# A written-out program table for the slots of a fused attention and maxout-FFN kernel, with two more steps' x transposed by DMA

## The chip, the cores and the metric

The kernel runs on one core of one Trainium2 chip. The metric is device time in microseconds of that core, as the median of several runs. Before the change it is 206.61 us (11 runs, 205.76 to 207.94).

## What is computed

Attention over 4 batches, 8 heads, 768 positions and head size 64, followed by a feed-forward layer on the 3072 tokens of 512 features that the attention gives.

```python
scores = q @ k.T / 8                       # per batch and head
keep   = causal                            # retrieval heads (0, 2, 6)
keep   = causal & (first 4 keys | last 64) # all other heads
a = softmax(where(keep, scores, -1e9)); x = a @ v
h = max(x @ w1, x @ w2, x @ w3); out = h @ w_out    # 512 -> 768 -> 512
```

Inputs and output are float32; the kernel computes in float16 with float32 accumulation.

## The kernel before, in words

**Steps and slots.** The 768 positions of a batch are two halves of 384, and the 8 heads are two groups of four. A step `t` (0 to 15) is one batch, one half of the queries and one group of heads: batch 0 has steps 0 to 3, and steps 2 and 3 are its second half. A half's scores are laid out in two or four PSUM-sized pieces `u` (`UNITS`); a slot is one `(t, u)`, so a first-half step has two slots and a second-half step four, 48 in all. Slots 0 to 3 belong to the opening; slots 4 to 47, and three more without scores, run in the loop at the end of the function.

**What a slot needs.** `scores` (L403) multiplies keys and queries on TensorE into PSUM, ScalarE takes the exponential into `pt` (L449), and `masks` (L456) multiplies the partly kept blocks on GpSimd (L472). In batch 0 the keys and queries are cast, turned on TensorE and copied (`cast_pair`, `turn_pair`, L159); from batch 1 on they are loaded as float32 by GpSimd's DMA queue (`load`, L171) and turned by VectorE's stream transpose (`turn`, L187, four for each head group). `prep_v` (L383) makes the float16 values: a cast to `va` (L389, on a chosen engine) and a product with the head flags to `vf` (L391, on GpSimd). `av` (L476) makes one pair of heads of a step: 12 or 30 small matmuls (L488), a reciprocal and a scaling on VectorE (L496, L498), which give `x`. FFN matmuls need `x` turned into `xT`: for the steps in `BY_DMA` (4 to 14) `av` issues a transposing DMA from SyncE (L507), for the others `turn_x` (L513) takes three TensorE transposes (L520) and a copy (L524).

**The FFN as a filler.** When the last `x` of a half is issued, `turn_x` appends `ffn(b, half)` (L316) to a queue. That is a generator of 24 units: 18 of four matmuls each (L335, 128x384 out of `yy`), evicted by ScalarE (L343) or combined by VectorE's maximum (L346), and six half units of the output product (L361, copy L367, store L368 by SyncE). `fill(n)` takes `n` units off the queue. There are eight such FFNs.

**What sets the order.** The schedule is manual: each engine runs its instructions in the order in which the Python emits them, and so do the DMA queues of SyncE, ScalarE and GpSimd. `put` files a call under a slot and a place (0: ahead of the scores, "x": behind them, 1: between the two fills, 2: at the end), and the loop emits scores, calls and `pace(n)` units, half of them ahead of place 1. `sync_after` (L195) is a tiny DMA on SyncE that reads slot 8's `pt`; the value loads of batch 1, emitted behind it, therefore wait for that exponential.

**The opening.** Ten dummy matmuls (`idle_work`, L222) run while the first loads land; then steps 0 and 1 are done by hand, and four plus one units of the first FFN between them. Of the four weights, `load_weight` puts `w0t` to GpSimd's queue first, then the second half's first keys and queries, `w1t`, the others, `w2t`, the values, and `woutt`.

Of the kernel before, what the change touches and what calls it, by code (L numbers as in the profile page):

```python
# [1 line left out]

# [9 lines left out]
ALU = mybir.AluOpType  # L13
# [35 lines left out]
def kernel(  # L49
# [14 lines left out]
    nc = tc.nc  # L64
# [18 lines left out]
    NQ = H // G  # L83
    NT4 = B * 2 * NQ

    BY_DMA = range(NQ * 2, NT4 - 1)

    consts = ctx.enter_context(tc.tile_pool(name="consts", bufs=1))
    stage = ctx.enter_context(tc.tile_pool(name="stage", bufs=3))
# [14 lines left out]
    def where(t):  # L104
        bh, qd = divmod(t, NQ)
        return bh // 2, bh % 2, qd
# [25 lines left out]
    def cast_pair(half, hp, engines):  # L132
        cast[half, hp] = []
        for nm, src, op in zip(("kn", "qn"), staged.pop((half, hp)), engines):
            x = half16.tile([P, HB, 2, D], FP16, tag=nm, name=nm)
            op(out=x, in_=src.rearrange("p h j d -> p j h d"))
            cast[half, hp].append(x)
# [6 lines left out]
    def turn_pair(half, hp, *engines):  # L144
        if (0, hp // 2) not in KQs:
            KQs[0, hp // 2] = qkt.tile([P, 2, S, 2], FP16, tag="KQ", name="KQ")
        xs = cast.pop((half, hp))
        n = 2 // len(engines)
        for part, op in enumerate(engines):
            tr = bank([P, 1024], FP16, "tr")  # L150
            for i in range(n):
                for j in range(HB):
                    c = i * HALF + j * P
                    nc.tensor.transpose(
                        tr[:, c : c + P],
                        xs[part + i][:, j].rearrange("p h d -> p (h d)"),
                        ident,
                    )
            op(  # L159
                out=of_pair(hp)[  # L160
                    :, part : part + n, half * HALF : (half + 1) * HALF
                ].rearrange("p i (t j) -> p i t j", j=HB),
                in_=tr[:, 0 : n * HALF].rearrange("p (i j t) -> p i t j", i=n, j=HB),
            )
# [57 lines left out]
    def idle_work(n):  # L222
        sink = sps.tile([P, 2, 512], FP32, tag="st", name="st")
        for _ in range(n):
            nc.tensor.matmul(sink[:, 0, :], zero[:, 0:P], zero, start=True, stop=True)
# [41 lines left out]
    def read_flags():  # L267
        nc.vector.tensor_scalar(
            out=RT1, in0=ir32[:, 0 : 2 * H : 2], scalar1=0.0, scalar2=None,
            op0=ALU.not_equal,  # L270
        )
# [108 lines left out]
                queue.pop(0)  # L380


    def prep_v(t, i, op=None):  # L383
        b, half, qd = where(t)
        vs = staged_v[b, half]
        j, k0 = b % 2, half * HB
        hs = slice(4 * qd + 2 * i, 4 * qd + 2 * i + 2)
        vdst = va[j][:, hs, k0 : k0 + HB, 0:D]
        (op or nc.vector.tensor_copy)(out=vdst, in_=vs[:, hs])  # L389
        k0, k1 = ((0, 1), (1, 4))[half]  # L390
        nc.gpsimd.tensor_tensor(  # L391
            out=vf[j][:, hs, k0:k1, 0:D],
            in0=vs[:, hs, 0:1] if half == 0 else va[j][:, hs, k0:k1, 0:D],
            in1=far[:, hs, k0:k1].unsqueeze(3).to_broadcast([P, 2, k1 - k0, D]),
            op=ALU.mult,
        )
# [6 lines left out]
    def scores(t, u, pairs=(0, 1)):  # L403
# [43 lines left out]
        for x, st in sts.items():  # L447
# [5 lines left out]
            if not early:  # L453
                masks(t, i, u)

    def masks(t, i, u):  # L456
        b, half, qd = where(t)
        pt = pts[t, i]
        h0 = 4 * qd + 2 * i
        for at, u0, nu, cols, n, m0 in MASKED[half]:  # L460
            if at != u:
                continue
            m = mk[:, h0 : h0 + 2, m0 : m0 + n]
            if nu == 1 and len(cols) == 1:
                x = pt[:, u0, :, cols[0] : cols[0] + n]
            elif nu == 2:
                x = pt[:, u0 : u0 + 2, :, cols[0] : cols[0] + n]
                m = m.unsqueeze(1).to_broadcast([P, 2, 2, n])
            else:
                x = pt[:, u0].rearrange("p h (c n) -> p h c n", n=n)[:, :, 0:4:3]  # L470
                m = m.unsqueeze(2).to_broadcast([P, 2, 2, n])
            nc.gpsimd.tensor_tensor(out=x, in0=x, in1=m, op=ALU.mult)  # L472

    xs = {}

# [52 lines left out]
            queue.append(ffn(b, half))  # L528


    SLOTS = [(t, u) for t in range(NT4) for u in range(len(UNITS[where(t)[1]]))]

    def idle():
        idle_work(3)

    dve, act, pool = nc.vector.tensor_copy, nc.scalar.copy, nc.gpsimd.tensor_copy
    idle_work(8)
    read_flags()
    cast_pair(0, 0, (dve, act))
    head_flags()  # L540
    idle_work(2)
    head_masks(0, True)
    turn_pair(0, 0, dve, dve)
    cast_pair(0, 1, (pool, act))
    head_masks(1, True)
    turn_pair(0, 1, dve)
    cast_pair(0, 2, (act, pool))
    scores(0, 0, (0,))
    turn_pair(0, 2, dve)
    scores(0, 0, (1,))  # L550
    head_masks(2, True)
    scores(0, 1, (0,))
    cast_pair(0, 3, (pool, pool))
    load_weight(0)
    far_flags()
    turn_pair(0, 3, dve)
    head_masks(3, True)
    scores(0, 1, (1,))
    scores(1, 0, (0,))
    scores(1, 0, (1,))  # L560
    scores(1, 1, (0,))
    for i in range(2):
        prep_v(0, i, pool)
    for i in range(2):
        prep_v(1, i, dve)
    load_pairs(1, 0, 2, (nc.gpsimd, nc.gpsimd))
    av(0, 0)
    scores(1, 1, (1,))
    av(0, 1)
    load_weight(1)  # L570
    load_pairs(1, 2, 2, (nc.gpsimd, nc.gpsimd))
    av(1, 0)
    turn_x(0, 0, act)
    turn_x(0, 1, act)
    av(1, 1)
    turn_x(1, 0)
    load_weight(2)
    load_v(0, 1, (nc.gpsimd,) * HB)
    load_weight(3)
    turn_x(1, 1)  # L580
    for hp in range(2):
        cast_pair(1, hp, (dve, act))
    fill(4)
    for hp in range(2):
        turn_pair(1, hp, dve)
    for hp in range(NHP):
        head_masks(hp)
    fill(1)


    FIRST = 4
    work = {}

    def put(n, place, f, *args):
        work.setdefault((n, place), []).append(lambda: f(*args))

    for b in range(B):
        o = 12 * b
        for i in range(2):
            if b > 0:  # L600
                put(o + i, 2, prep_v, 2 * NQ * b, i, act if b == 1 else None)
                put(o + 2 + i, 2, prep_v, 2 * NQ * b + 1, i, act if b == 1 else None)
                put(o + i, 1, av, 4 * b - 1, i)
                put(o + 1 + i, "x", turn_x, 4 * b - 1, i)
                put(o + 2 + i, 1, av, 4 * b, i)
                put(o + 3 + i, "x", turn_x, 4 * b, i)
                put(o + 4 + i, 1, av, 4 * b + 1, i)
                put(o + 5 + i, "x", turn_x, 4 * b + 1, i)
            late = 1 if b == 0 else 0
            put(o + (8 if late else 6) + i, late, prep_v, 4 * b + 2, i, act if b == 0 else None)  # L610
            put(o + 10 + i, 2, prep_v, 4 * b + 3, i, act if b == 0 else None)
            put(o + 8 + late + i, 1, av, 4 * b + 2, i)
            put(o + 9 + late + i, "x", turn_x, 4 * b + 2, i)
        if b + 1 < B:
            put(o + (5 if b == 0 else 3), 0, load, b + 1, 0)
            put(o + (8 if b == 0 else 5), 0, load, b + 1, 1)
            if b == 0:
                put(9, 0, lambda: sync_after(pts[3, 1][0:1, 0, 0, 0:2]))
            put(o + (9 if b == 0 else 7), 0, load_v, b + 1, 0)
            put(o + 11, 0, load_v, b + 1, 1)  # L620
            for qd in range(2):
                for x in range(2):
                    for p in range(2):
                        if b == 0:
                            n, place = 10 + 2 * qd + x, "x" if qd else (0, "x")[p] if x == 0 else 0
                        else:
                            n, place = o + 8 + 2 * qd + x, 1
                        put(n, place, turn, b + 1, qd, x, p)
    for i in range(2):
        put(12 * B + i, 1, av, NT4 - 1, i)  # L630
        put(12 * B + 1 + i, "x", turn_x, NT4 - 1, i)
        put(5, 1, cast_pair, 1, 2 + i, (dve, act))
        put(6 + i, 1, turn_pair, 1, 2 + i, dve)

    def pace(n):
        return 2.4 if n < 8 else 1.6 if n < 11 else 3.0 if n < 14 else 3.6 if n < 20 else 4.0

    due = 0.0
    for n in range(FIRST, len(SLOTS) + 3):
        def do(place):  # L640
            for f in work.pop((n, place), ()):
                f()

        do(0)
        if n < len(SLOTS):
            scores(*SLOTS[n])
        do("x")
        due += pace(n)
        part = int(due / 2)
        fill(part)  # L650
        due -= part
        do(1)
        part = int(due)
        fill(part)
        due -= part
        do(2)
    assert not work
    while queue:
        fill(1)
# [33 lines left out]
```

## Time and profile before

| | |
|---|---|
| median of 11 runs | 206.61 us (205.76 to 207.94) |
| the profiled execution | 207.26 us, with a span of 205.5 us from first to last instruction |
| busy: TensorE, VectorE, ScalarE, GpSimd | 191.6, 126.6, 124.9, 128.9 us |
| granted TensorE clock | 1.00 |
| read from HBM, written | 25.17 MB, 6.29 MB |
| stores of the output, from issue to landing | 2.4 us (median of 23) |

The page adds up busy time by engine, follows the chain of work that ended last back from the end, and lists groups of instructions by source line with their mean duration and with what ended the idle time before them. Matmuls overlap in the array, so the mean duration of one (326 ns for 128x384) is not its pitch: in the timeline groups of four start 0.65 us apart. A row such as `xT<-x` names the tile written and the tile read.

### The profile page before, as it was taken

How to read it: one execution, taken by the hardware profiler on the slowest of the kernel's cores; microseconds unless marked ns; L12 is line 12 of the kernel's file. 1: busy time of each engine (PE TensorE's matmuls, PEld its weight loads, DVE VectorE, ACT ScalarE, POOL GpSimd, SP SyncE). 2: the span in 40 equal slices, each digit the busy share in tenths (PEclk: the TensorE clock that was granted, in tenths of full speed). 3: DMA queues.
4: the chain of work that ended last, by engine and by line, in shares of the span. 5: the costliest groups of instructions: out<-in, count | busy, mean ns of one | idle time of the engine just before them, and what ended most of it. 6: DMA issues, size and time to landing. Idle time of an engine off the chain costs nothing.

```text
span 205.5 us, 5167 instructions
## 1 busy us (share of the span) xinstructions
PE 191.6 (93%) x2071; PEld 108.4 (53%) x2071; DVE 126.6 (62%) x257; ACT 124.9 (61%) x190; POOL 128.9 (63%) x156
## 2 busy tenths in 40 slices
PE   7698699888899999999999999999899999999992
PEld 2455354546465456455656466465455465665552
DVE  3886687597656538994696268983546234753540
ACT  3492797868586865746657676656377775514221
POOL 3489569869997834489987906589908816800000
PEclk9999999999999999999999999999999999999999
DMA  5989999999539993803389952603211130012004
GB/s 184 251 130 213 243 245 214 211 221 242 161 56 196 140 249 92 153 3 92 124 149 187 177 184 48 129 19 122 72 22 38 60 117 19 3 51 105 0 0 153
DMA packets 41581, 26.08 MB, mean 127 GB/s; under 512 B 31894, under 2 KB 36566, under 8 KB 41558
## 3 DMA queue, kind: packets, MB, share of 16 engines
q1 hardware_dynamic: 35542, 14.62, 31.8%
q0 software_dynamic: 4784, 10.23, 26.1%
q10 hardware_dynamic: 1232, 0.92, 1.4%
q8 instruction: 16, 0.26, 0.5%
q14 instruction: 7, 0.06, 0.1%
HBM read 25.17 MB, written 6.29 MB: 153 GB/s over the span
## 4 chain that ended last, share of the span: by engine, by line
PE 67%; DMA 19%; DVE 8%; POOL 2%; issue 1%; ACT 1%; ACTq 0%; SPq 0%; POOLq 0%; DVEq 0%
PE yy L335 35%; PE yy L361 13%; PE st L438 8%; PE oacc L488 8%; DMA kq<-in_k_dram 7%; DVE KQ L187 5%; DMA w1t<-in_moe_w_dram 4%; PE yst L335 3%; DMA qs<-in_q_dram 3%; DMA vs<-in_v_dram 3%; DMA xT<-x 2%; DVE x L498 1%; PE yst L361 1%; POOL vf L391 1%; DVE acc L346 1%
## 5 line engine op out<-in xcount | busy, mean ns | idle before, releaser
L472 POOL TENSOR_TENSOR pt<-pt,mk 128x512 f16<-128x512 f16 x84 | 89.7, 1094 | 29.1 <-ACT pt L449 27.8
L449 ACT ACTIVATE pt<-st 128x1024 f16<-128x1024 f32 (+3 forms) x99 | 83.0, 894 | 27.7 <-PE st L438 25.5
L346 DVE TENSOR_TENSOR acc<-yy,acc 128x384 f16<-128x384 f32 x45 | 25.2, 561 | 23.4 <-PE yy L335 17.1
L335 PE MATMUL yy<-xT,w0t 128*128 128x384 f16 x180 | 36.6, 326 | 1.0 <-DMA xT<-x 1.0
L335 PE MATMUL yy<-xT,w2t 128*128 128x384 f16 x180 | 36.6, 326 | 0.0
L335 PE MATMUL yy<-xT,w1t 128*128 128x384 f16 x180 | 36.3, 326 | 0.1
L361 PE MATMUL yy<-woutt,hT 128*128 128x512 f16 (+1 forms) x138 | 32.7, 375 | 0.3 <-DVE hT L346 0.3
L343 ACT CAST acc<-yy 128x384 f16<-128x384 f32 x45 | 21.4, 482 | 18.2 <-PE yy L335 12.3
L438 PE MATMUL st<-KQ 32*128 32x384 f16 (+5 forms) x560 | 28.8, 279 | 1.8 <-DVE KQ L187 1.0
L346 DVE TENSOR_TENSOR hT<-yy,acc 128x384 f16<-128x384 f32 x45 | 25.1, 558 | 6.0 <-PE yy L335 3.4
L488 PEld LDWEIGHTS <-pt 128*128 128x128 f16 x672 | 24.9, 97 | 5.8 <-issue 1.0
L187 DVE STREAM_TRANSPOSE KQ<-kq 128x384 f32<-128x384 f32 x24 | 25.0, 1138 | 0.5 <-DMA kq<-in_k_dram 0.5
L488 PE MATMUL oacc<-va,pt 128*128 128x65 f16 x352 | 25.1, 193 | 0.0
L335 PEld LDWEIGHTS <-w1t 128*128 128x128 f16 x192 | 17.5, 97 | 14.0 <-issue 3.5
L496 DVE RECIPROCAL rc<-oacc 128x6 f32<-128x6 f32 x32 | 6.1, 191 | 30.4 <-PE oacc L488 30.1
L335 PEld LDWEIGHTS <-w2t 128*128 128x128 f16 x192 | 17.3, 98 | 12.2 <-issue 1.4
L335 PEld LDWEIGHTS <-w0t 128*128 128x128 f16 x192 | 17.5, 97 | 11.5 <-issue 0.9
L438 PEld LDWEIGHTS <-KQ 32*128 32x128 f16 (+1 forms) x560 | 12.1, 93 | 21.8 <-issue 15.6
L488 PE MATMUL oacc<-vf,pt 128*128 128x65 f16 x320 | 21.4, 193 | 0.7 <-POOL vf L391 0.7
L367 ACT COPY ot<-yy 128x512 f32<-128x512 f32 x22 | 13.0, 590 | 14.7 <-PE yy L361 13.9
L361 PEld LDWEIGHTS <-hT 128*128 128x128 f16 x150 | 13.4, 98 | 15.0 <-issue 1.4
L391 POOL TENSOR_TENSOR vf<-va,far 128x384 f16<-128x384 f16 x16 | 13.2, 827 | 11.6 <-DVE va L389 9.5
(67 smaller groups left out, 130.3 us busy)
## 6 DMA issues: line engine op xcount, KB each, us to landing
out_dram<-ot SPq DMA_DIRECT2D x23, 256.0 KB, 2.4
vs<-in_v_dram SPq DMA_DIRECT2D x21, 256.0 KB, 4.8
kq<-in_k_dram POOLq DMA_DIRECT2D x6, 384.0 KB, 6.8
kq<-in_q_dram POOLq DMA_DIRECT2D x6, 384.0 KB, 8.5
qs<-in_q_dram ACTq DMA_DIRECT2D x4, 192.0 KB, 5.7
ks<-in_k_dram SPq DMA_DIRECT2D x4, 192.0 KB, 4.9
w0t<-in_moe_w_dram POOLq DMA_DIRECT2D x1, 768.0 KB, 7.1
ks<-in_k_dram POOLq DMA_DIRECT2D x2, 384.0 KB, 6.9
```

What stands on the lines that cost most here:

```text
L187: nc.vector.transpose(out=dst.rearrange("c (p j) -> c j p", j=n)[:, j0:j1], in_=src.rearrange("c (j i) -> c j i", i=R),)
L335: nc.tensor.matmul(yy[:, 0:HALF], w_t[wi][:, ks, ni * P : (ni + 1) * P], xT[b, half][ks].rearrange("p a t -> p (a t)"), start=(ks == 0), s ...
L343: nc.scalar.copy(out=acc[ni], in_=yy[:, 0:HALF])
L346: nc.vector.tensor_tensor(out=dst, in0=yy[:, 0:HALF], in1=acc[ni], op=ALU.max)
L361: nc.tensor.matmul(yo[:, 0:n], hT[ns][:, tb * P : (tb + 1) * P], woutt[:, ns, c : c + n], start=(ns == 0), stop=(ns == NNB - 1),)
L367: op(out=ot[:, c : c + n], in_=yo[:, 0:n])
L391: nc.gpsimd.tensor_tensor(out=vf[j][:, hs, k0:k1, 0:D], in0=vs[:, hs, 0:1] if half == 0 else va[j][:, hs, k0:k1, 0:D], in1=far[:, hs, k0:k ...
L438: nc.tensor.matmul(sts[g // m][:, g % m, c0 : c0 + n * P], KQ[rows, 0, ki * P : (ki + 1) * P], KQ[rows, 1, t0 : t0 + n * P], start=(c0 == ...
L449: nc.scalar.activation(out=pts[t, i][:, u, h0 : h0 + m, 0:w], in_=st[:, :, 0:w], func=AF.Exp, scale=sc,)
L472: nc.gpsimd.tensor_tensor(out=x, in0=x, in1=m, op=ALU.mult)
L488: nc.tensor.matmul(o[:, qi, hl, 0 : D + 1], pt[:, u, hl, c : c + P], vv[:, 2 * hp + hl, ki, 0 : D + 1], start=(idx == 0), stop=(idx == len ...
L496: nc.vector.reciprocal(out=rc, in_=o[:, :, :, D])
```

## The change

A literal table takes the place of `put` and `pace`: one row for each slot from 4 on, with its FFN units, a flag, and four lines of calls (ahead of the scores, behind them, between the fills, at the end). With the flag the scores of the two head pairs are emitted apart, with a third of the units between them if that comes to a whole one. Most rows repeat the former places with calls moved by a slot or less. `BY_DMA` now holds steps 2 and 15 too. `prep_v` takes an engine for each of its two operations, and three masks go to VectorE. The opening's casts, flags and values are spread over the engines in another way, both scores of steps 0 and 1 stand ahead of the first `av`, and seven units instead of five are taken in it.

```diff
-    BY_DMA = range(NQ * 2, NT4 - 1)
+    BY_DMA = (2, 4, 5, 6, 7, 8, 9, 10, 11, 12, 13, 14, 15)
...
-        (op or nc.vector.tensor_copy)(out=vdst, in_=vs[:, hs])
+        op(out=vdst, in_=vs[:, hs])
-        nc.gpsimd.tensor_tensor(
+        vf_engine.tensor_tensor(
...
+    MASK_ON_DVE = ((3, 1, 3), (6, 0, 1), (7, 0, 1))
-            nc.gpsimd.tensor_tensor(out=x, in0=x, in1=m, op=ALU.mult)
+            engine = nc.vector if (t, i, u) in MASK_ON_DVE else nc.gpsimd
+            engine.tensor_tensor(out=x, in0=x, in1=m, op=ALU.mult)
...
     idle_work(8)
+    cast_pair(0, 0, (act, act))
     read_flags()
-    cast_pair(0, 0, (dve, act))
     head_flags()
-    idle_work(2)
     head_masks(0, True)
     turn_pair(0, 0, dve, dve)
+    idle_work(2)
     cast_pair(0, 1, (pool, act))
...
-    cast_pair(0, 2, (act, pool))
+    cast_pair(0, 2, (pool, pool))
...
+    turn_pair(0, 3, dve)
     far_flags()
-    turn_pair(0, 3, dve)
-    head_masks(3, True)
+    prep_v(0, 0, dve, nc.gpsimd)
     scores(0, 1, (1,))
+    prep_v(0, 1, dve, nc.vector)
+    prep_v(1, 0, dve, nc.vector)
     scores(1, 0, (0,))
+    scores(1, 1, (0,))
+    prep_v(1, 1, dve, nc.gpsimd)
+    load_pairs(1, 0, 2, (nc.gpsimd, nc.gpsimd))
     scores(1, 0, (1,))
-    scores(1, 1, (0,))
-    for i in range(2):
-        prep_v(0, i, pool)
-    for i in range(2):
-        prep_v(1, i, dve)
-    load_pairs(1, 0, 2, (nc.gpsimd, nc.gpsimd))
+    scores(1, 1, (1,))
     av(0, 0)
-    scores(1, 1, (1,))
+    load_weight(1)
     av(0, 1)
...
+    PROGRAM = (
+        (2.4, True, "", "", "cast 1 2 dd", "cast 1 3 ap"),
+        (2.4, False, "load 1 0", "", "", ""),
+        (2.0, False, "pair 1 2", "", "", "pair 1 3"),
+        (2.2, False, "load 1 1", "", "", ""),
+        (2.2, True, "", "", "v 2 0 dd", "gate"),
+        (1.6, True, "v 2 1 ap, load_v 1 0", "", "av 2 0", ""),
+        (1.6, True, "", "x 2 0, turn 1 0 0 0, turn 1 0 0 1", "av 2 1, turn 1 0 1 1", "v 3 0 pp"),
+        (3.0, False, "turn 1 0 1 0, load_v 1 1", "x 2 1", "", "v 3 1 ap"),
+        (3.6, False, "", "turn 1 1 0 0, turn 1 1 0 1, turn 1 1 1 1, av 3 0", "", "v 4 0 pd"),
+        (3.0, False, "av 3 1", "", "", "turn 1 1 1 0, v 4 1 ad"),
+        (3.6, False, "x 3 0, x 3 1", "", "av 4 0", ""),
+        (3.6, False, "", "v 5 0 ad, x 4 0, av 4 1", "", "v 5 1 ap, load 2 0"),
...
+        (3.6, False, "av 7 0, x 7 0, av 7 1", "", "", "v 8 1 dp"),
+        (4.0, False, "", "v 9 0 dp", "av 8 0, x 7 1", ""),
...
+        (4.0, False, "", "", "av 11 0", "v 12 0 dp"),
+        (4.2, False, "x 11 0, av 11 1", "", "", "v 12 1 dp"),
+        (4.8, False, "", "v 13 0 dp, x 11 1", "av 12 0", ""),
...
+        (4.0, False, "", "", "av 15 0", ""),
+        (4.0, False, "x 15 0, av 15 1", "", "", ""),
+        (4.0, False, "", "x 15 1", "", ""),
+    )
...
+    for (units, apart, *lines), slot in itertools.zip_longest(PROGRAM, SLOTS[FIRST:]):
+        run(lines[0])
+        if slot and apart:
+            scores(*slot, (0,))
+            part = int(due + units / 3)
+            fill(part)
+            due -= part
+            scores(*slot, (1,))
+        elif slot:
+            scores(*slot)
+        run(lines[1])
+        due += units
         part = int(due / 2)
         fill(part)
         due -= part
-        do(1)
+        run(lines[2])
         part = int(due)
         fill(part)
         due -= part
-        do(2)
+        run(lines[3])
```

In a row, `d`, `a` and `p` stand for VectorE, ScalarE and GpSimd; `v 4 0 pd` is `prep_v(4, 0)` with the cast on GpSimd and the product on VectorE, `pair` is `turn_pair`, `x` is `turn_x`, and `gate` is `sync_after`.

## The prediction

> **What bounds the kernel now.** I read the page's busy times first, then busy time by stage, then what each engine waited for, and last the chain of waits and single stretches of the timeline.
>
> ```profile
> PE 191.6 (93%) x2071; PEld 108.4 (53%) x2071; DVE 126.6 (62%) x257; ACT 124.9 (61%) x190; POOL 128.9 (63%) x156
> ```
>
> TensorE is busy for 93% of the span; nothing else passes 63%. The four stages below are mine: 18 us is where the first FFN unit starts, 53 us where the second FFN does, 198 us where the last output product begins. In each row the second number is the length; TensorE's busy time follows, and the last three are clock, DMA share and GB/s.
>
> ```profile
> 0.00:18.00 18.00, 13.97 (x142) 7.43 (x143) 12.97 (x37) 10.11 (x18) 10.69 (x26) 1.00 0.85 190
> 18.00:53.00 35.00, 29.86 (x343) 16.82 (x341) 25.51 (x49) 25.51 (x40) 28.36 (x33) 1.00 1.10 232
> 53.00:198.00 145.00, 143.86 (x1566) 81.96 (x1567) 87.12 (x170) 87.74 (x130) 89.81 (x99) 1.00 0.46 95
> 198.00:205.50 7.50, 3.89 (x24) 2.15 (x22) 0.98 (x3) 1.55 (x3) 0.00 (x0) 1.00 0.29 105
> ```
>
> So from 53 to 198 us TensorE lacks only 1.1 us; there an edit pays only if it takes work or that 1.1 us off TensorE. From 18 to 53 us it lacks 5.1 us, while the DMA engines are full (share 1.10, 232 GB/s). The first 18 us lack 4.0, of which 1.26 is the start. The last row is not touched.
>
> ```profile
> PE tr L520 <- DVE x L498: 1.7, 4, 0.6
> PE tr L154 <- ACT acc L343: 1.6, 1, 1.6
> PE tr L154 <- POOL kn L136: 1.6, 1, 1.6
> ...
> PE yy L335 <- DMA xT<-x: 1.0, 1, 1.0
> ```
>
> The waits are many and short, and only one of them, 1.0 us for a transposed x, lies behind 53 us. What fixes the 53 us is the chain of waits there:
>
> ```profile
> 25.56 15.02 DMA kq<-in_k_dram
> ...
> 40.60 1.14 DVE KQ L187
> ...
> 44.02 2.00 DVE KQ L187 x2
> ...
> 50.07 2.00 DVE KQ L187 x2
> ...
> 52.99 0.34 PE tr L520 x3
> ```
>
> The keys of batch 1, issued at 25.56, land at 40.58 behind everything queued ahead of them; VectorE turns them, with small work between, until 52.06, and then step 3's last x is turned and the second FFN begins (53.17 in the timeline). From there TensorE has work without end. So the new time is: when that FFN starts, plus what TensorE has left to do, plus its stalls.
>
> **Part 1, the opening (up to 18 us).** GpSimd loses two value casts (0.56 and 0.58) and two of four products ahead of the second half's loads, so these can be issued about 1.2 us sooner than 15.15. But in 14 to 16 us the DMA share is already 1.16, and `w0t` is ahead in the same queue until 17.4; `w0t` itself still waits for the last casts, whose input lands at about 9.3. Only small holes (shares 0.93 and 0.91 in 16 to 18 and 20 to 22 us) can be filled: 0.3 us of 1.2. VectorE gains two casts (0.57 each) and two products; its chain of four casts, two products and four scalings of 0.72 moves the first FFN unit from 18.06 to about 18.9. That is hidden: TensorE next stands until 22.51 for ScalarE, whose evictions are queued behind casts waiting for loads that land at about 21.1. Without that cover it costs 0.9. The two further FFN units taken there end at one that needs `w1t` (landing 25.3): TensorE may wait about 0.8 us in front of the scores, where it idled before anyway. The parted scores change nothing on TensorE: its new order shows no unit between the pairs in any of the flagged slots.
>
> **Part 2, slots 4 to 13.** The total of TensorE is the same, less six transposes of step 2. GpSimd's cast of the last queries now stands ahead of the issue of batch 1's keys and holds it until those land, some 2 us; the keys wait 15.0 us in a full queue, so it costs nothing until the delay nears that. The second group's loads are issued two masks (2 x 1.16) sooner into the same full queue: nothing. On VectorE, between the keys' landing and the second FFN stand now: eight turns of 1.02 (8.2), three pairs of reciprocal and scaling (2.1), one mask, two products, two xT copies of 0.38 (0.8). The mask has no row on VectorE; its nearest are the head-mask builds (0.33 to 0.59 for 512 elements), a product is about 0.3 by the same rows for 128 elements. The sum is 12.3 us, against 12.0 of work and 1.1 of idle before: 40.6 + 12.3 = 52.9 for 53.4 before, less up to 0.3 from the loads.
>
> One rule speaks against the mask and the products on VectorE. The Trainium skill, page "SBUF — State Buffer", section "SBUF: two separate sides", says that VectorE with two SBUF inputs and GpSimd hold one port pair exclusively, for a whole instruction. By it each such operation can wait for a GpSimd mask of 1.16: three of them between 40 and 53 us make 52.9 into up to 56.4. No row of two SBUF inputs on VectorE beside a busy GpSimd exists here; the nearest, value casts on VectorE, took 0.565 on average against 0.51 at least while GpSimd was 63% busy. I take 0.1 each and keep 3.5 for the range.
>
> Step 2's x goes through SyncE's queue, behind the batch-1 values, which landed at 50.08 (ScalarE's cast waited for them), with a store between its two transposes. At 1.19 us a transpose (its issue) and 1.0 for 256 KB at 250 GB/s the second lands at 50.1 + 1.2 + 1.0 + 1.2 = 53.5, less 0.3. The second FFN's second matmul needs it: about 53.1, against 53.33 before. Between 52.6 and 53.1, I take a start earlier by 0.4. The bounds are 1.7 earlier and 3 later; see the rivals.
>
> **Part 3, from the second FFN on.** The one stall:
>
> ```profile
> 142.86 0.65 PE L335 MATMUL yy<-xT,w0t 128*128 128x384 f16 x3
> 144.47 0.32 PE L335 MATMUL yy<-xT,w0t 128*128 128x384 f16 x1 [0.96 <-DMA xT<-x]
> ```
>
> The fourth matmul of a new FFN waited for step 11's last x: its `av` ended at 139.39, and only 3.5 us of other work (two output products, one score slot, one short `av`) stood between. In the new order this gap holds a short score slot, one FFN unit, three output products, a score slot and a short `av`: 0.6 + 0.65 + 3 x 1.29 + 0.66 + 0.37 = 6.2 us for a need of about 5.0. Also, two stores no longer stand ahead of the transposes in SyncE's queue. Gain 1.0. Step 7's gap grows from 3.6 to 5.5 in the same way.
>
> Step 15's x no longer takes six TensorE transposes: three start within 0.17, so 6 x 0.057 = 0.34, and I take 0.3. Here a page says more: "TensorE: Matmul & The Clock Gate", section "PE-mode transpose", gives about 275 ns in a kernel. That would make 1.65 us; but 219 ns is this trace's duration too, and what the queue behind pays is the pitch, 0.057. The DMA in their place needs 0.8 for VectorE and 2.3 to 3.3 to land (those of step 14), under 4.5 + 0.5 us of units and products still ahead. Without that cover it would cost 3 us.
>
> Small gaps between units in this stage, evictions that come late, sum to 1.6 us beside the stall. The turns of batches 2 and 3 are now mostly one at a time, not in pairs that keep VectorE for 2.1 us; masks of steps 6 and 7 leave GpSimd, value casts swap engines at equal price (0.51 to 0.57). I take 0.4 of 1.6, between 1.0 lost and 1.0 gained. Loads and stores keep their order to within a slot, and nothing idles for them there.
>
> **Sum.** The profiled execution took 207.26 (span 205.5 and 1.76 around it). 0.4 + 1.0 + 0.3 + 0.4 = 2.1 gives 205.2; it lay 0.65 above the median of 206.61, so the median becomes 204.5.
>
> **The rivals.** *The opening runs ahead:* the loads do move by 1.2 us and VectorE has no idle, so the second FFN starts 1.6 us sooner: 203.2. For it: the new VectorE chain has no wait in it. Against: a DMA share of 1.10. *The stalls move:* pacing that starves or overfills TensorE elsewhere takes back the stall's 1.0 and the 0.4, and the opening gives nothing: 206.3. *Slower, step 2's transposes land late:* next to software-queue loads a transpose took 9.9 us to land, not 2.4:
>
> ```profile
> xT<-x SPq DMA_TRANSPOSE x1, 9.9
> ```
>
> Issued at about 47 us after the store, the second would land at 57, and the second FFN would start 3.6 us later: 206.6 - 1.7 + 3.6 = 208.5. It decides from a landing past 55, where it eats the other 1.7. Against it: the software queue's loads were through by 47.2, and what is ahead then is counted above. *The change does nothing on TensorE:* excluded but for the parted scores, since the emitted order differs throughout.
>
> **How the numbers follow.** A measurement here tells about 0.3% (0.6 us) from no change. Forecast 204.5 (own range 203.4 to 205.7): 0.54; ahead, 203.2: 0.16; stalls move, 206.3: 0.17; late, 208.5: 0.13. Of the third about a fifth is faster by over 0.6. So faster 0.73, within 0.14, slower 0.13. The range, 202.8 to 207.0, leaves out most of the late case and the far end of the early one.
>
> **What would show it.** Right: the second FFN's first unit at 52.3 to 53.2 us; no wait of `yy` for `xT<-x` near 143 us; no L520 rows of steps 2 and 15; from 53 us on the same TensorE work with less than 1 us idle. Part 2 wrong: `yy` waiting on `xT<-x` near 53 us, or VectorE masks of over 1 us. Part 3 wrong: idle TensorE ahead of the last FFN, near 183 us. The forecast fails if that second start moves by over 1.5 us either way.

## The result, and the profile after

The changed kernel took 203.89 us (median of 12 runs, 202.67 to 205.44) against 206.61 (47 runs beside the changed kernel): a ratio of 0.9881, 95% interval 0.9856 to 0.9907. Executions that lie more than 1.5% above the fastest of their kernel (three of e1, one of e6) are left out of all ratios and medians of the experiments. The profiled execution of the changed kernel took 203.81 us, with a span of 202.1.

The profile after, busy times (share of the span, instructions):

```profile
PE 190.0 (94%) x2059; PEld 108.7 (54%) x2059; DVE 130.4 (65%) x260; ACT 124.8 (62%) x188; POOL 125.6 (62%) x151
```

The same four stages as before (start:end and length, then TensorE, its weight loads, VectorE, ScalarE, GpSimd, clock, DMA share, GB/s):

```profile
0.00:18.00 18.00, 14.51 (x144) 7.81 (x145) 13.07 (x39) 10.39 (x19) 10.77 (x25) 1.00 0.95 208
18.00:53.00 35.00, 30.20 (x343) 17.03 (x340) 27.80 (x52) 24.34 (x36) 27.24 (x31) 1.00 1.04 219
53.00:198.00 145.00, 144.78 (x1574) 83.64 (x1573) 89.14 (x168) 89.71 (x134) 87.54 (x97) 1.00 0.48 100
198.00:202.10 4.10, 0.52 (x5) 0.22 (x3) 0.42 (x1) 0.32 (x1) 0.00 (x0) 1.00 0.40 140
```

TensorE has 12 instructions fewer, the transposes of steps 2 and 15. Behind 53 us it lacks 0.2 us, not 1.1, and by 198 us only 5 matmuls are left instead of 24. What TensorE waited for, longest first (total, times, longest):

```profile
PE tr L525 <- DVE x L503: 1.8, 4, 0.6
PE yy L336 <- DMA w1t<-in_moe_w_dram: 1.5, 1, 1.5
...
PE oacc L493 <- POOL pt L477: 0.8, 1, 0.8
PE st L439 <- DVE KQ L188: 0.7, 1, 0.7
```

The wait of `yy` for `xT<-x` is gone; instead the first FFN's w1t units wait 1.5 us, far ahead of the second FFN. The start of that FFN in TensorE's timeline:

```profile
50.73 0.34 PE L525 MATMUL tr<-ident,x 128*128 128x128 f16 x3 [0.55 <-DVE x L503]
51.77 0.63 PE L439 MATMUL st<-KQ 32*128 32x384 f16 x16 [0.70 <-DVE KQ L188]
52.34 0.83 PE L336 MATMUL yy<-xT,w0t 128*128 128x384 f16 x4
```

52.34 us, for 53.17 before. What comes last ahead of it is still VectorE: the scores at 51.77 waited 0.70 us for the last turn of batch 1's keys and queries (`KQ`). The kernel before has the same wait of 0.7, with one for VectorE's `x` behind it. The chain of waits that ends last, though, passes this place through GpSimd's masks, and reaches TensorE at the next `av`, 1.0 us behind the FFN's first matmul:

```profile
45.93 1.29 POOL pt L477
...
52.18 1.12 POOL pt L477
53.35 0.45 PE oacc L493 x9
```

So VectorE sets the start in both kernels, and GpSimd's masks follow it closely.

The span can be split at the second FFN's start. Before: 53.17 to it and 152.3 behind it. After: 52.34 and 149.8. So 0.8 us of the 3.4 come ahead of it and 2.6 behind, where the number of matmuls is nearly the same (1589 before, 1587 after). The table gives both parts for every kernel; they are of one profiled execution, while the median is of all. The kernel before and e5, e6 and e10 have equal code up to there, and yet they started this FFN anywhere from 51.50 (e6) to 53.17 us (before), so a start of one execution settles little. The length behind it is the steadier number. Where a clock is named in the table, TensorE ran at half of it for a while behind the start, and the figure is what that lost.

| kernel | second FFN at | from there to the end | median us |
|---|---|---|---|
| before | 53.17 | 152.3 | 206.61 |
| after | 52.34 | 149.8 | 203.89 |
| e1, after with the old opening | 53.27 | 149.4 | 204.89 |
| e2, before with the new opening | 51.14 | 153.6 | 206.85 |
| e5, earlier `av` on before | 53.14 | 151.2 | 205.76 |
| e6, single turns on before | 51.50 | 151.4 | 205.41 |
| e10, e5 and e6 | 51.78 | 151.1 | 205.78 |
| e9, after with the old pace | 50.86 | 152.1, 1.5 by the clock | 205.0 |
| e11, after with all masks on GpSimd | 52.78 | 150.8, 1.2 by the clock | 205.16 |
| e4, after with step 2 on TensorE | 52.39 | 150.5, 1.5 by the clock | 205.86 |
| e7, after with the gap filled | 52.00 | 149.8 | 203.43 |
| e8, e4 with the gap filled | 52.76 | 149.1 | 204.56 |

### The profile page after: what moved, and what is told of

Read it like the earlier page. It is cut to its first block, busy times and chain, and to the rows that moved or that the text cites. A ratio compares the mean times of both kernels' runs of the same rounds, so it can differ in the third digit from the quotient of the medians.

```text
span 202.1 us, 5148 instructions
## 1 busy us (share of the span) xinstructions
PE 190.0 (94%) x2059; PEld 108.7 (54%) x2059; DVE 130.4 (65%) x260; ACT 124.8 (62%) x188; POOL 125.6 (62%) x151
## 4 chain that ended last, share of the span: by engine, by line
PE 76%; DMA 8%; POOL 7%; DVE 3%; ACT 2%; issue 1%; SPq 1%; DVEq 0%; ACTq 0%
PE yy L336 41%; PE yy L362 13%; PE st L439 9%; PE oacc L493 9%; DMA w1t<-in_moe_w_dram 5%; POOL pt L477 4%; PE yst L336 3%; DMA ks<-in_k_dram 3%; POOL vf L392 1%; ACT pt L450 1%; DMA out_dram<-ot 1%; DVE KQ L160 1%; PE yst L362 1%; DVE mk L293 1%; ACT ot L368 1%
## 5 line engine op out<-in xcount | busy, mean ns | idle before, releaser
L477 POOL TENSOR_TENSOR pt<-pt,mk 128x512 f16<-128x512 f16 (+1 forms) x81 | 86.6, 1093 | 31.3 <-ACT pt L450 31.3
L336 PE MATMUL yy<-xT,w0t 128*128 128x384 f16 x180 | 36.1, 327 | 0.1
L493 PEld LDWEIGHTS <-pt 128*128 128x128 f16 x672 | 23.8, 97 | 5.5 <-issue 1.4
L503 DVE TENSOR_TENSOR x<-oacc,rc 128x384 f16<-128x384 f32 x32 | 17.8, 558 | 1.1
```

Source lines behind the costliest of these rows:

```text
L336: nc.tensor.matmul(yy[:, 0:HALF], w_t[wi][:, ks, ni * P : (ni + 1) * P], xT[b, half][ks].rearrange("p a t -> p (a t)"), start=(ks == 0), s ...
L477: engine.tensor_tensor(out=x, in0=x, in1=m, op=ALU.mult)
L493: nc.tensor.matmul(o[:, qi, hl, 0 : D + 1], pt[:, u, hl, c : c + P], vv[:, 2 * hp + hl, ki, 0 : D + 1], start=(idx == 0), stop=(idx == len ...
L503: nc.vector.tensor_tensor(out=x, in0=o[:, :, :, 0:D], in1=rc.unsqueeze(3).to_broadcast([P, HB, 2, D]), op=ALU.mult,)
```

## The experiments

The theory at the start was that of the prediction: the stall near 143 us and the small gaps behind 53 us give about 1.4 us, the opening little. The rival was that the opening leads, and that what lies behind it follows from there. Later two more questions came up: what the table's unit counts do, and why the granted clock halves in some executions.

**e1: the changed kernel with the old opening.** Slots 4 on are as in the changed kernel.

```diff
-    cast_pair(0, 0, (act, act))
     read_flags()
+    cast_pair(0, 0, (dve, act))
...
-    prep_v(0, 1, dve, nc.vector)
-    prep_v(1, 0, dve, nc.vector)
     scores(1, 0, (0,))
+    scores(1, 0, (1,))
     scores(1, 1, (0,))
...
+    for i in range(2):
+        prep_v(0, i, pool, nc.gpsimd)
+    for i in range(2):
+        prep_v(1, i, dve, nc.gpsimd)
```

> The changed kernel with the opening of the kernel before (all up to slot 4), table and DMA steps as changed. Theory (most of the gain lies behind 53 us; the opening moves the second FFN's start by 0.8 us at most, and the later slots' work on VectorE and GpSimd sets that start in any case): about 204.3, 0.4 above the changed kernel. Rival (the opening's earlier loads made the 0.8 us and more): 205 or above, with the second FFN's first unit at 53.2 us or later.

Ratio 0.9921 (0.9884 to 0.9958), median 204.89 us: 1.0 more than the changed kernel. The intervals of the two ratios overlap, and of the executions at a clock of 0.996 or more the medians are 204.31 and 203.66, which is 0.65. In its profile the second FFN began at 53.27, 0.9 later, and behind it the length is 149.4, for 149.8 after. So inside this change the opening is worth some 0.6 to 1.0 us, between the two expectations, and not clear of the noise. What is lost lies ahead of the second FFN.

**e2: the kernel before with the new opening alone**, the opposite edit.

> The kernel before with the changed opening alone; slots from 4 on, their paces and the DMA steps as before. Theory: 206.2, 0.4 below the kernel before, the second FFN's first unit between 52.7 and 53.2 us, and the wait of 1.0 us for the transposed x near 143 us still there. Rival (the opening does it): 205.0 or less.

Ratio 1.0015 (0.9992 to 1.0039): nothing. TensorE's waits behind 50 us in e2:

```profile
PE oacc L488 <- POOL pt L472: 1.2, 2, 1.0
PE yy L335 <- DMA xT<-x: 1.0, 1, 1.0
PE st L438 <- DVE KQ L187: 0.2, 1, 0.2
```

The FFN began at 51.14, but TensorE then stood 1.2 us (at 53.0 and 60.6) for GpSimd's masks, a wait that the kernel before has nowhere behind 50 us, and the stall near 143 us is still there. In this execution a lead of 2.0 us came down to 0.8 in the span, and in the median nothing is left. That the new order of the slots behind is what keeps the lead in the changed kernel fits e1 and e2, and is not shown by itself.

**e3: step 15 back on TensorE**, `BY_DMA` without 15.

> The changed kernel with step 15's x turned by TensorE again. By the pitch of a TensorE transpose (0.057 us, six of them): 0.3 us more, 204.2. By the skill's 275 ns each: 1.6 us more, 205.5. If the two copies on VectorE also hold up evictions: up to 0.8 more.

Median 204.0 of 6 (202.88 to 205.02), ratio 0.9874 (0.9832 to 0.9916), against 203.89: 0.1, not told from nothing. The three executions at a clock of 0.997 and above took 202.88 to 203.20; those of the changed kernel at such a clock have a median of 203.66. So the 1.65 of the 275 ns rule is excluded. The 0.3 predicted is too small to be seen or excluded in six executions.

**e4: step 2 back on TensorE**, `BY_DMA` without 2.

> The changed kernel with step 2's x turned by TensorE again. Theory (VectorE's chain between 40 and 52 us sets the start of the second FFN; two copies of 0.38 us more stand on it): 0.4 to 0.8 us more, 204.3 to 204.7. Rival (the transposing DMAs behind the values were the limit of that start): the same or up to 0.5 us less.

205.86 us, ratio 0.9976 (0.9948 to 1.0004), 2.0 more than the changed kernel, and every one of 12 executions had a mean clock of 0.983 to 0.992. Busy time of the engines by the microsecond in e4; the clock is the third number from the end:

```profile
48.00:49.00 1.00, 0.14 (x6) 0.00 (x0) 1.00 (x3) 0.91 (x2) 1.00 (x3) 1.00 1.21 282
49.00:50.00 1.00, 0.31 (x3) 0.17 (x3) 0.95 (x5) 0.58 (x2) 1.00 (x2) 1.00 1.09 220
50.00:51.00 1.00, 0.37 (x4) 0.17 (x3) 0.97 (x2) 0.00 (x0) 1.00 (x3) 1.00 1.21 249
51.00:52.00 1.00, 0.31 (x8) 0.22 (x12) 1.00 (x2) 0.00 (x0) 1.00 (x2) 1.00 0.88 251
52.00:53.00 1.00, 1.00 (x18) 0.43 (x7) 0.66 (x3) 0.45 (x1) 1.00 (x1) 0.52 0.18 51
53.00:54.00 1.00, 1.00 (x10) 0.66 (x9) 0.00 (x0) 1.00 (x2) 0.49 (x2) 0.50 0.00 0
54.00:55.00 1.00, 1.00 (x13) 0.66 (x11) 0.41 (x2) 0.86 (x2) 1.00 (x2) 0.50 0.00 0
55.00:56.00 1.00, 1.00 (x6) 0.54 (x5) 0.54 (x2) 0.00 (x0) 1.00 (x2) 0.77 0.00 0
```

TensorE is busy for 0.14 to 0.37 of each microsecond from 48 to 52, then it gets half the clock for 3.4 us (0.48 + 0.50 + 0.50 + 0.23 lost is 1.7 us), just when the second FFN fills it. One such stretch makes a mean clock of 0.99, as in this execution; in the seven executions at 0.983 two fit, as in e11's trace, which has 6.8 us at half clock. Which part of the 2.0 is the transposes and which the clock, e7 and e8 tell apart.

**e7: the changed kernel with the gap filled.** Eight dummy matmuls of 128x512, whose results nothing reads, go in front of, between and behind the transposes of step 3 (the lines that define `idle` are left out here).

```diff
-        (3.0, False, "av 3 1", "", "", "turn 1 1 1 0, v 4 1 ad"),
-        (3.6, False, "x 3 0, x 3 1", "", "av 4 0", ""),
+        (3.0, False, "av 3 1", "", "", "turn 1 1 1 0, v 4 1 ad, idle 2"),
+        (3.6, False, "x 3 0, idle 3, x 3 1, idle 3", "", "av 4 0", ""),
```

> The changed kernel with eight dummy 128x512 matmuls, which compute nothing used, where TensorE waits between 48 and 52 us (two behind the scores of slot 13, three behind each turned x of step 3). Theory of the clock: TensorE's clock is halved for 3.4 us in those executions in which that stretch looked idle, at 1.5 to 1.7 us each, in about half of them; filled, every execution keeps a clock of 0.997 or more there, and the median falls from 203.9 to 203.4 with a narrower spread. Rival (the clock falls for another reason, or the dummies delay the work): clocks of 0.99 remain, or 0.3 to 0.6 us more.

203.43 us (202.63 to 203.82), ratio 0.9818 (0.9781 to 0.9854), with a clock of 0.996 to 1.0 in all six. Of the changed kernel's own 12 executions four had 0.988 to 0.990 and took 205.08 to 205.44, the other eight a median of 203.66. None of six against four of twelve could still be chance; e8 settles it.

**e8: e4 with the same dummies.**

> Step 2's x on TensorE as in the earlier run (205.86, clock 0.983 to 0.992 in all 12 executions), with the same eight dummy matmuls. Theory of the clock: 203.6 to 204.2 with a clock of 0.997 or more, so that step 2's DMA is worth at most 0.5 us by itself and the rest was the clock. Rival (the turned x itself costs 2 us on VectorE or TensorE): 205.5 or more, with a clock of 1.0.

204.56 us, ratio 0.9889 (0.9849 to 0.9928), clock 0.998 and above in all. The same stretch in e8:

```profile
48.00:49.00 1.00, 0.98 (x11) 0.26 (x10) 1.00 (x2) 0.60 (x2) 1.00 (x3) 1.00 0.92 224
49.00:50.00 1.00, 0.01 (x1) 0.01 (x1) 0.95 (x4) 0.88 (x2) 1.00 (x1) 1.00 1.18 265
50.00:51.00 1.00, 1.00 (x7) 0.42 (x8) 0.96 (x4) 0.00 (x0) 1.00 (x3) 1.00 1.12 218
...
53.00:54.00 1.00, 1.00 (x18) 0.74 (x17) 0.02 (x1) 1.00 (x2) 0.63 (x2) 1.00 0.01 2
```

With work in it the stretch keeps the clock, in six of six where e4 lost it in twelve of twelve. So of e4's loss 1.3 us are the clock (205.86 - 204.56), and with the gap filled step 2's DMA is worth 1.1 (204.56 - 203.43). The two make more than e4's 2.0 because the changed kernel itself loses 0.46 where the gap is open. TensorE's waits from 40 to 60 us in e8 and then in e7:

```profile
PE tr L525 <- DVE x L503: 1.4, 2, 1.0
PE st L439 <- DVE KQ L188: 0.4, 1, 0.4
```

```profile
PE oacc L493 <- POOL pt L477: 0.8, 1, 0.8
```

1.8 us against 0.8. Only 0.4 of the 1.8 is the wait of step 2's own transposes, the first of these rows; the second row is step 3's, which TensorE takes in both kernels:

```profile
43.33 0.34 PE L525 MATMUL tr<-ident,x 128*128 128x128 f16 x3 [0.40 <-DVE x L503]
49.99 0.34 PE L525 MATMUL tr<-ident,x 128*128 128x128 f16 x3 [1.02 <-DVE x L503]
```

VectorE's `x` comes later there: in e8 VectorE also copies step 2's `xT` (0.34 at 46.03), and the mask ahead of that took 1.05 us for 0.58 in the changed kernel. The second FFN starts at 52.76 for 52.00. How the 1.1 divides between copy and mask is not shown.

**e5: the kernel before with step 11's and step 7's last `av` ahead of the scores of its slot.**

```diff
-                put(o + i, 1, av, 4 * b - 1, i)
+                put(o + i, 0 if i and b > 1 else 1, av, 4 * b - 1, i)
```

> The kernel before with one move: in batches 2 and 3 the second pair's av of the last step of the batch before (steps 7 and 11) stands ahead of the slot's scores, not behind the first fill, so that 5.5 us of other work instead of 3.5 covers its transposing DMA. Theory: the wait of 1.0 us near 143 us goes and nothing takes its place: 205.7, 0.9 to 1.0 below the kernel before. Rival (the wait moves to the next thing): within 0.3 of the kernel before.

205.76 us, ratio 0.994 (0.9915 to 0.9965), 1.08 under the kernel before: the stall's size. No wait of TensorE is left behind 60 us.

**e6: the kernel before with the turns of batches 2 and 3 one at a time.**

```diff
-                            n, place = o + 8 + 2 * qd + x, 1
+                            n, place = o + 8 + 2 * qd + x, (1, 2)[p]
```

> The kernel before with the eight stream transposes of each of batches 2 and 3 taken one at a time, one behind the first fill of a slot and one at its end, not in pairs. Theory (the small gaps of 0.15 to 0.2 us between FFN units come from pairs that hold VectorE for 2.1 us): 0.6 to 0.9 us less, 205.8. Rival (the gaps come from the paces or from ScalarE): no change.

Ratio 0.9941 (0.9909 to 0.9973). In its profile the stall is gone too, but a new wait came in. TensorE's waits behind 55 us in e6:

```profile
PE yy L335 <- DVE hT L346: 0.9, 2, 0.4
```

The gaps that it was meant to close did get smaller. Two groups of four FFN matmuls, in the kernel before and then in e6, where also one of the two new waits is shown:

```profile
85.98 0.81 PE L335 MATMUL yy<-xT,w0t 128*128 128x384 f16 x4
86.79 0.81 PE L335 MATMUL yy<-xT,w1t 128*128 128x384 f16 x4
```

```profile
84.15 0.81 PE L335 MATMUL yy<-xT,w0t 128*128 128x384 f16 x4
84.80 0.81 PE L335 MATMUL yy<-xT,w1t 128*128 128x384 f16 x4
...
89.60 0.81 PE L335 MATMUL yy<-xT,w2t 128*128 128x384 f16 x4 [0.43 <-DVE hT L346]
```

The starts are 0.81 us apart before and 0.65 in e6, the pitch of a group. Take, from 60 to 200 us, every FFN matmul that follows another FFN matmul or an `av` and starts more than 0.04 us later than the usual pitch behind it. Together they lose 1.6 us before, beside the stall, and 0.65 in e6, beside two new gaps of 0.6 each at the places of the `hT` wait. So e6 closes the small gaps by about 1 us and gives that back there; what it keeps is the stall. Why step 11's last x landed after 2.3 us there and after 4.1 us in the kernel before stays open: SyncE issued the same transfers in the same order.

**e10: e5 and e6 together on the kernel before.**

> The kernel before with both single moves, early av (which alone gave 205.76) and single turns (205.53). If each removes a loss of its own (the wait near 143 us; the gaps behind paired turns): 204.5, a ratio of 0.988 to the kernel before, as much as the whole change. If both remove the same wait: 205.5, a ratio of 0.994.

205.78 us, ratio 0.997 (0.9936 to 1.0004), no more than either alone, and the 0.9 for `hT` is still there. Both take away the same wait; the small gaps are down to 0.4 us here, against 1.6 in e5, and the same two gaps of 0.6 stand against that.

**e9: the changed kernel with the old unit counts.** All calls stay where the table has them; only the number of FFN units of each slot is that of before.

```diff
-    for (units, apart, *lines), slot in itertools.zip_longest(PROGRAM, SLOTS[FIRST:]):
+    def pace(n):
+        return 2.4 if n < 8 else 1.6 if n < 11 else 3.0 if n < 14 else 3.6 if n < 20 else 4.0
...
+    for n, ((_, apart, *lines), slot) in enumerate(itertools.zip_longest(PROGRAM, SLOTS[FIRST:]), FIRST):
+        units = pace(n)
```

> The changed kernel with its order of calls, but the units of each slot as the kernel before paced them (2.4, 1.6, 3.0, 3.6, 4.0). Theory (the gain behind 53 us comes from where the calls stand, the wait near 143 us above all): within 0.4 of the changed kernel, 203.5 to 204.3. Rival (the table's unit counts remove the small gaps of 1.2 us): 205.

205.0 us, ratio 0.9921 (0.9892 to 0.995): the rival, not my theory. With clocks of 0.996 and above its median is 204.94 against 203.66, so it is not the clock. Busy time from 60 to 198 us, first after, then e9:

```profile
60.00:198.00 138.00, 137.87 (x1497) 79.63 (x1495) 85.20 (x159) 84.58 (x125) 80.54 (x90) 1.00 0.47 99
```

```profile
60.00:198.00 138.00, 137.21 (x1487) 78.73 (x1485) 82.69 (x159) 82.95 (x123) 79.09 (x87) 1.00 0.46 97
```

In 138 us TensorE was busy 0.66 us less and got 10 matmuls less done, with two waits for late evictions among the causes. TensorE's waits behind 55 us in e9:

```profile
PE yy L336 <- DVE acc L347: 0.5, 1, 0.5
PE yy L336 <- DVE hT L347: 0.2, 1, 0.2
```

The first of these stands at 89.33 us, in the same place as the wait at 89.60 in e6. Without the 1.5 us of the clock the length behind the second FFN's start is 150.6, 0.8 more than after. So the trace places 0.7 to 0.8 of the 1.3 there; where the rest is lost is not shown.

**e11: the changed kernel with all masks on GpSimd**, `MASK_ON_DVE = ()`.

> The changed kernel with the three masks back on GpSimd. Theory (GpSimd's chain of masks ends with VectorE's turns near 52 us, and three masks of 1.16 are more than VectorE pays for them): 0.3 to 1.0 us more, 204.2 to 204.9. By the skill's port rule (each mask on VectorE waits for a GpSimd mask): no loss, or 0.5 less.

205.16 us of 11, ratio 0.9915 (0.9889 to 0.9942). TensorE's waits from 40 to 60 us in e11:

```profile
PE oacc L493 <- POOL vf L392: 0.8, 1, 0.8
PE oacc L493 <- POOL pt L477: 0.6, 1, 0.6
PE st L439 <- DVE KQ L188: 0.5, 1, 0.5
```

The three masks are worth 1.3 us. The waits for GpSimd have grown from 0.8 to 1.4, which is half of it. This profiled execution ran at half clock for some 7 us around the second FFN's start (mean clock 0.983), but six of the others had 0.997 or more and still a median of 205.2, so the clock does not explain the rest, which stays open.

**e12: e7 with one mask more on VectorE** and the two value products of step 4 back on GpSimd.

> The changed kernel with the eight dummy matmuls (203.43 with those alone) and, besides, the mask of step 3's first pair on VectorE, where VectorE waits 0.55 us for the second pair's exponential, and in exchange the two value products of step 4 on GpSimd. If VectorE's chain sets the second FFN's start: 0.2 to 0.5 less, 203.0. If GpSimd's masks do: the same or a little less. If the port is held: up to 0.8 more.

203.12 us (202.73 to 205.01), ratio 0.9832 (0.9788 to 0.9876). The waits for `pt` and `KQ` are gone from its profile, and the time is that of e7 within the spread. One of the six executions had a clock of 0.992 and took 205.01, with the dummies in place. By their medians e7 and e12 lie below both kernels.

## Why the prediction was right, and where its steps were not

The forecast of 204.5 lies 0.6 us above the 203.89 measured. The mechanism was right: a second FFN that starts somewhat earlier (52.34, inside the 52.3 to 53.2 named), no stall, and the same TensorE work with fewer gaps. The sizes are right in their total more than one by one: three terms came out larger than forecast, one was not seen and the clock took some back, so that the distance is as small as 0.6 is in part luck.

- **The stall near 143 us, -1.0: right.** It is gone after, and e5 alone gave 1.08.
- **The opening, -0.4: rather too small, and its cover was missed.** e1 puts it at 0.6 to 1.0 in the changed kernel, e2 at nothing in the old one. The prediction counted VectorE's chain to the second FFN, and that chain does set the start (the wait of 0.70 for `KQ`). Its check against the kernel before is off by 0.3: 40.6 and 12.0 of work and 1.1 of idle make 53.7, not 53.4. It left out GpSimd's masks, which follow so closely that a lead is lost to them: 0.8 us of waiting at 47.28 us after, 1.2 in e2. The masks moved to VectorE (e11: 1.3) give room at that place; that they alone let the lead through was not tried. The wait for `w1t` was 1.5, not 0.8, and was hidden; the delay of batch 1's keys (issued at 27.90 instead of 25.56) cost nothing, as said.
- **Step 2's x, priced as a risk: it is a gain.** SyncE's queue in the timeline after:

```profile
44.62 2.73 SPq L512 DMA_TRANSPOSE xT<-x  x1
...
48.15 1.22 SPq L512 DMA_TRANSPOSE xT<-x  x1
```

  The second transposing DMA was issued at 48.15 and landed after 2.3 us, not at 53.2 to 53.5, because the step's `av` stood early enough to go ahead of the last value loads. e8 against e7 gives 1.1 for it. The late-landing rival (208.5) did not occur.
- **Masks on VectorE, 0.33 to 0.59 plus 0.1: right in duration, but their gain was put at nothing.** The prediction took them as a cost to VectorE alone; e11 shows 1.3 us in their favour. The line's durations (min, median, max in ns) after:

```profile
L477 DVE TENSOR_TENSOR pt<-pt,mk x3: 424/426/578, 45.6 to 77.0; 128x512 f16<-128x512 f16 x3
```

  But the reason given for the 0.1 was weak. It took value casts on VectorE as 0.51 at the least; over the whole trace of before they were 331/352/2120 ns, and the longest one stood beside two GpSimd masks. VectorE's row and GpSimd's row in the timeline of before:

```profile
103.76 2.12 DVE L389 CAST va<-vs 128x384 f16<-128x384 f32 x1
```

```profile
103.37 2.28 POOL L472 TENSOR_TENSOR pt<-pt,mk 128x512 f16<-128x512 f16 x2
```

  The cast ended at 105.88, 0.2 behind the masks. That fits the exclusive port that the Trainium skill, page "SBUF — State Buffer", section "SBUF: two separate sides", describes. The page names operations with two SBUF inputs and those in what it calls a 2-port perf mode; which mode this cast, with one SBUF input, ran in is not shown. Operations with two SBUF inputs were not always cheap either. A product with the flags in e1 and then a mask in e8, both on VectorE beside a busy GpSimd:

```profile
49.79 1.13 DVE L392 TENSOR_TENSOR vf<-vs,far 128x128 f16<-128x128 f32 x1
```

```profile
45.06 1.05 DVE L477 TENSOR_TENSOR pt<-pt,mk 128x512 f16<-128x512 f16 x1
```

  In the changed kernel such products took 0.28 to 0.48 and that mask 0.58. So 0.1 each was the good case, and the 3.5 kept for the range was not idle. No run isolates the cause.
- **Step 15's x, -0.3: not seen** (e3).
- **Small gaps, -0.4: the mis-sized term, with half of the cause.** Behind the second FFN's start 2.6 us went. The stall takes 1.0 to 1.1 of it. The small gaps, 1.6 us before, are 0.55 after, counted as in e6, so they gave about 1.1. The prediction named the single turns, and e6 and e10 show that these close most of the gaps. What it left out is that at the old unit counts two evictions then come late and take as much again (two gaps of together 1.2 us in e6, 1.0 in e9); the table's unit counts keep them away, and no gap after is longer than 0.27. e9 puts the counts at 1.3 us by the medians at a full clock. That they suit what VectorE can take in each slot is a reading of the waits for `acc` and `hT`, not a test.
- **The clock: not foreseen.** It takes some 1.6 us from a third of the executions of the changed kernel (205.26 against 203.66; one of those at a full clock took 205.12 too), and e7 has a median 0.46 lower.

Taken out singly, opening, step 2's DMA, unit counts and masks cost 1.0, 2.0, 1.1 and 1.3 us; with the stall that is more than the 2.7 of the whole. Three of them meet in the stretch from 45 to 53 us, so they need not add up, and the 2.0 of step 2 holds 1.3 of clock.

## What to carry to other kernels

Split the span where the filler work starts, and compare the length behind it between kernels, since the start itself moved by 1.7 us at equal code. Add up the small gaps too, and not only the listed waits: e6 closed 1 us of gaps and opened as much in two others, which its time alone hides. A lead at the start of a pipeline can be lost at the engine next in the chain (here GpSimd's masks), so trying an opening alone can show nothing. How many filler units stand in each slot deserves as much care as where the calls stand: at equal calls it was worth 1.1 to 1.3 us of 204.

## What the runs showed of the hardware that was not expected

In e4 a thin stretch of 4 us on TensorE (busy 0.14 to 0.37 of each, never idle for a whole one) was followed by half the clock for 3.4 us, and all twelve executions have a mean clock of 0.983 to 0.992. Shorter stretches can do: in the traces of e9 (0.34 and 0.34 from 48 to 50 us) and e3 (0.47 and 0.34 from 49 to 51) the clock halved too. In e1 (0.57, 0.33 and 0.30 from 50 to 53) and in the profiled execution of the changed kernel (0.45 and 0.30 from 50 to 52) it did not, and of the twelve executions of the latter it did in four. So no threshold on the busy share follows from these runs.

The Trainium skill, page "TensorE: Matmul & The Clock Gate", section "What's actually happening", gives a free-running window of about 3.4 us, and the clock in the traces agrees. In e3, e4, e9 and e11 full clock had been granted for 47.79, 47.79, 44.37 and 44.37 us when it halved, which is 14, 14, 13 and 13 times 3.413, and it stayed halved for 3.41, 3.41, 3.41 and 6.83. Such a fixed grid, laid differently over each execution, would also make the borderline case vary, which no run here isolates.

With eight dummy matmuls the clock held in 17 of 18 executions (e7, e8, e12), and they cost less than they saved (203.43 against 203.89, and 204.56 against 205.86 with step 2 on TensorE).
